# Attention with decay and two feed-forward blocks on one core: weight words to ScalarE, an x product queued behind the q and k remainders, two first-layer products behind the last second-layer product

## The chip, the cores and the metric

The kernel runs on one core of a Trainium2 chip. The metric is the device time of one execution in microseconds, taken over several runs; the profile is one further execution, recorded by the hardware profiler.

## The reference

Four batches of eight heads with 576 positions and 64 features attend causally, with a decay in the exponent; the result goes through two feed-forward blocks. Cut to what matters:

```
scores = q @ k.T / 8 + (cum[i] - cum[j])       # cum = cumsum(log f), causal
attn   = exp(scores - max) / sum               # [4, 8, 576, 576]
x      = (attn @ v) as [2304, 512]
h      = x @ w_in                              # w_in  [512, 2048]
g      = h * tanh(softplus(h))
x2     = g @ w_out                             # w_out [2048, 512]
a, b   = x2 @ w1, x2 @ w2                      # [512, 1024] each
out    = ((a * b) @ w3) @ w_out2               # w3 and w_out2 are multiplied first
```

The weights arrive as 64-bit floats and are handled as pairs of 32-bit words.

## The kernel before

Every float32 product is done in three TensorE passes: an operand is split into a rounded high part and a remainder, and MM_PAIRS (line 60) multiplies high by high, high by remainder and remainder by high. A helper `split` (line 91) makes the two parts; the remainder on POOL (GpSimd) is `pool_sub` (line 102, its instruction is line 108). POOL in the rows is GpSimd, ACT is ScalarE, DVE is VectorE, PE is TensorE with PEld for its weight loads, SP is the queue that issues every DMA.

**Phase A** (`phase_a`, line 685) runs 16 pairs of heads. A pair has nine slots, so there are 144 slots and some more at the end. In a slot the scores of one unit go to PE, the transposes of the unit before it follow, DVE takes the row minimum (line 425), ACT takes the exponential (line 429), and ACT and DVE split the transposed probabilities (lines 502 and 504). In slots 3 and 5 of the next pair the products with v run (`pv`, line 533; `x_rows`, lines 545 and 546; `x_parts`, line 548, whose product with the inverse row sums R is line 551). The heads to come are prepared by `prep_qk` (line 336): ACT copies (lines 348 and 349), then the remainders of k and of q on POOL. v is split by ACT and POOL in `prep_v` (lines 374 and 378).

PE's free time is filled with products that are ready: first w3 times w_out2, later the first layer of the batches that are done (`l1_unit`, line 610; ACT copies the finished bank in line 617 and a DMA stores it, line 618). `plan` (line 663) hands out how many of these go in each slot; `run_filler` queues each behind the slot's scores. A timeline-based scheduler then orders each engine's instructions by readiness and priority, within the bounds that `behind` (an instruction after which something may be issued) and `high_priority` set.

The slots also **convert weights**. A job is: `cv_load` (line 111) issues the load of 512 KB into one of two buffers; `cv_exp` (line 120) multiplies the upper words by a power of two; `cv_bits` (line 134) puts the bits together on DVE (lines 140 to 142); then the tile is split (w3t, w_in) or stored to DRAM (`cv_store`, line 148). Keys are t for w3t, i for w_in, u for w_out and v for w1 and w2. For t and i `cv_exp` is one ScalarE activation of 128x512 (line 132); for u and v it is two GpSimd instructions of 128x256 (line 130). The job's load stands in slot s, `cv_exp` and `cv_bits` in slot s + 1, the store in s + 2 (function `job`, line 734). The u and v jobs begin at slot 72 and come every 2.35 slots.

**Phase B** (`phase_b`, line 978) first runs 16 steps: a step computes g for one feature tile of block 0 (`mish_step`: DVE lines 890, 891 and 896, ACT lines 875 to 884, POOL line 892, the split of g in ACT line 94 and POOL line 108), runs two first-layer products of the last batch (l1[2c] and l1[2c+1]), splits a tile of w1 or w2 (`w12_split`), and runs the second-layer product of the step before (`l2`, line 932). After the last step `l2(15)` closes block 0, `x2_parts` (lines 940 and 941) splits its four banks, and eight blocks of third-layer, second-layer and last products (lines 951, 932 and 971) follow. The third layer takes turns on four PSUM banks, two of which are those of the first layer.

Of the kernel before, what the change touches and what calls it, by code (L numbers as in the profile page):

```python
# [13 lines left out]
AF = mybir.ActivationFunctionType  # L14
ALU = mybir.AluOpType
# [24 lines left out]
HB = 3  # L40
CV = 2
HP_L1 = 50
CV_POOL = "uv"
HP_ATT = 100
HP_SM = 200
HP_PV = 50
# [4 lines left out]
W_OUT_STEP = 2.35  # L51
# [5 lines left out]
W_OUT_SLOT = 72  # L57
# [5 lines left out]
def f32(ap):  # L63
    return ap.bitcast(F32)
# [4 lines left out]
F64_EXP = 2.0 ** -112  # L69
# [3 lines left out]
class Kernel:  # L73
# [28 lines left out]
    def pool_sub(self, lo, raw, hi):  # L102

        n = lo.shape[-1]
        k = -(-n // 320)
        for i in range(k):
            c = slice(n // k * i, n // k * (i + 1))
            self.nc.gpsimd.tensor_tensor(lo[..., c], raw[..., c], f32(hi[..., c]), ALU.subtract)  # L108


    def cv_load(self, key, src, where=None):
# [8 lines left out]
    def cv_exp(self, key):  # L120
        raw = self.cv[key][0]
        if key[0] in "to":
            t = self.x_tile(f"cv{key}", F32)[:, :512]
        else:
            t = self.att.tile([128, 512], F32, name=f"cv{key}", tag="cv", bufs=CV)
        self.cv[key][1] = t
        hw = raw.rearrange("p (n w) -> p n w", w=2)[:, :, 1]
        if key[0] in CV_POOL:
            for c in (slice(0, 256), slice(256, 512)):
                self.nc.gpsimd.tensor_scalar(t[:, c], f32(hw[:, c]), F64_EXP, None, ALU.mult)  # L130
        else:
            self.nc.scalar.activation(t, f32(hw), AF.Copy, scale=F64_EXP)

    def cv_bits(self, key):

# [200 lines left out]
    def prep_qk(self, h, step):  # L336


        nc = self.nc
        raw = self.raw[h]  # L340
        t1, t2 = self.tset(h)
        d0 = 64 if h % 2 else 0
        qs, ks = self.qk_cols(h)
        qd = slice(qs.start + d0, qs.stop + d0)
        kd = slice(ks.start + d0, ks.stop + d0)
        qr, kr = raw[:, h % 2 == 0], raw[:, h % 2]
        if step == 0:
            nc.scalar.copy(t1[:, d0:d0 + 2 * S], raw.rearrange("p w s -> p (w s)"))
            nc.scalar.copy(t2[64:128, qd], qr[64:128])
        elif step == 1:  # L350
            self.pool_sub(t2[64:128, kd], kr[64:128], t1[64:128, kd])
        else:
            self.pool_sub(t1[0:64, qd], qr[0:64], t1[0:64, qd])

    def load_v(self, p):
        nc = self.nc
# [328 lines left out]
    def phase_a(self):  # L685
# [43 lines left out]
        misc, conv = {}, {}  # L729

        def at(s, fn, *a):
            misc.setdefault(s, []).append((fn, a))

        def job(s, key, src, fin, *a):
            at(s, self.cv_load, key, src)
            conv.setdefault(s + 1, []).append(key)
            at(s + 2, fin, *a)

        jobs = [(f"t{f}{q}", self.cols(self.w3t, f, q), self.w3_split, f, q) for f in range(1, 8) for q in range(2)]
        for i, j in enumerate(jobs):  # L740
            job(int(W3_STEP * i), *j)
        jobs = [(f"i{m}", self.cols(self.w_in, m), self.win_split, m) for m in range(DFF // 128)]
        for i, j in enumerate(jobs):
            job(W_IN_SLOT + int(W_IN_STEP * i), *j)
        for i in range(32):
            f = i % 16
            if i < 16:
                key, src, dst = f"u{f}", self.rows(self.w_out, f), self.wo_scr
            else:
                key, src, dst = f"v{f}", self.cols((self.w1, self.w2)[f % 2], f // 2), self.w12_scr  # L750
            job(W_OUT_SLOT + int(W_OUT_STEP * i), key, src, self.cv_store, key, dst[f])
        for p in range(NPAIR):
            s = 9 * p
            if p == 0:
# [20 lines left out]
        for s in range(nslot + 7):  # L775
            if s in L1_S[:3]:
                self.filler.extend(self.l1_all(L1_S.index(s)))
            n = cnt[s]
            with self.tc.high_priority(offset=HP_ATT):
                if s < nslot:  # L780
                    self.pe = self.scores(s)
                if 0 <= s - T_LAG < nslot:
                    self.transposes(s - T_LAG)
                    act = self.pt_parts(s - T_LAG, False)
            if s < nslot:
                with self.tc.high_priority(offset=HP_SM):
                    act = self.softmax_a(s)
            with self.behind(act):
                for key in conv.get(s, []):
                    self.cv_exp(key)  # L790
            k = n // 2
            self.run_filler(k)
            if 0 <= s - T_LAG < nslot:
                with self.tc.high_priority(offset=HP_ATT):
                    dve = self.pt_parts(s - T_LAG, True)
            with self.behind(dve):
                for key in conv.get(s, []):
                    self.cv_bits(key)
            with self.behind(act):
                for fn, a in misc.get(s, []):  # L800
                    fn(*a)
            self.run_filler(n - k)
            if s >= 9:
                p, i = divmod(s - 9, 9)
                with self.tc.high_priority(offset=HP_PV):
                    if i == PV_AT[0]:
                        self.pv(2 * p)
                        self.x_rows(2 * p)
                    elif i == PV_AT[1]:
                        self.pv(2 * p + 1)  # L810
                        self.x_rows(2 * p + 1)
                        self.x_parts(p)
        self.run_filler(len(self.filler))
        self.psp.__exit__(None, None, None)
        self.attp.__exit__(None, None, None)
# [110 lines left out]
    def l2(self, c):  # L926
        f = c % 16
        g = self.g.pop(c)
        mm = self.nc.tensor.matmul
        for e in range(4):  # L930
            for k, (a, b) in enumerate(MM_PAIRS):
                mm(self.xb(e), self.wo[f][:, 512 * a + 128 * e:512 * a + 128 * e + 128],  # L932
                   g[:, TB * b:TB * b + TB], start=f == 0 and k == 0, stop=f == 15 and k == 2)

    def x2_parts(self, j):
        nc = self.nc
        self.x2 = []
        for e in range(4):
            t = self.x_tile(f"x2_{j}_{e}")
            nc.scalar.copy(t[:, :TB], self.xb(e))  # L940
            nc.vector.tensor_tensor(t[:, TB:], self.xb(e), f32(t[:, :TB]), ALU.subtract)
            self.x2.append(t)
# [35 lines left out]
    def phase_b(self):  # L978
        self.hl, self.mt, self.g = {}, {}, {}
        self.late_pool()  # L980
        self.hst = [self.x_tile(f"hst{i}", F32) for i in range(2)]
        l1 = [self.l1_unit(B - 1, m, half) for m in range(16) for half in range(2)]

        def run(steps):
            for _, fn in steps:
                fn()


        for f in range(2):
            self.wout_load(f)  # L990
        for c in range(4):
            self.h_load(c)
        self.m_min(0)
        self.m_exp(0)
        self.m_n(0)
        self.m_min(1)
        for c in range(16):
            self.w12_load(c)
            self.wout_split()
            self.mish_step(c)  # L1000
            run(l1[2 * c])
            if c >= 1:
                self.w12_split()
            run(l1[2 * c + 1])
            if c >= 1:
                self.l2(c - 1)
            if c + 2 < 16:
                self.wout_load(c + 2)
            if c % 2 == 0:
                self.wp_load(c // 2)  # L1010
        self.w12_split()
        self.l2(15)
        self.x2_parts(0)
        for j in range(NBLK):
            self.ab = []
            for f in range(8):
                more = j + 1 < NBLK
                c = 16 * (j + 1) + 2 * f
                if more:
                    self.mish_step(c)  # L1020
                self.l3(j, f)
                self.ab_parts(j, f)
                if more:
                    if f:
                        self.l2(c - 1)
                    self.mish_step(c + 1)
                    self.l2(c)
            if more:
                self.l2(16 * (j + 1) + 15)
            for e in range(4):  # L1030
                self.final(j, e)
                if e == 0 and more:
                    self.x2_parts(j + 1)
# [52 lines left out]
```

## Time and profile before

| | us |
|---|---|
| median of three runs | 1069.72 |
| lowest and highest run | 1068.0, 1072.33 |
| the profiled execution's own time | 1069.25 |
| its span, first to last instruction | 1067.1 |
| PE busy in the span | 965.8 (91%) |
| DVE busy | 770.7 (72%) |
| ACT busy | 633.0 (59%) |
| POOL busy | 598.2 (56%) |

The page cuts the span into 40 equal slices and gives each engine's busy share in tenths, so that a stage shows as a run of digits. Phase A fills about the first 18 of them, the first 16 steps of phase B the next four, the eight blocks the rest. Busy time says how much work an engine has; what a wait costs is read from the rows of the stage in which it stands.

### The profile page before, as it was taken

Reading aid. Unit: us, or ns where it says so; the run is one execution under the profiler, and the core shown is the slowest. Engines: PE = TensorE matmul, PEld = TensorE weight load, DVE = VectorE, ACT = ScalarE, POOL = GpSimd, SP = SyncE. Lnnn points to the kernel's source line nnn. Section 1 sums busy time; section 2 is a strip of 40 time slices with the busy share of each in tenths; the row PEclk is TensorE's granted clock in tenths of the full one; section 3 lists DMA queues with packets and bytes.
Section 4 is the critical chain, followed back from the end, with each engine's and each line's share of the span. In section 5 each row is a group of like instructions: output and inputs, shape, how many; then the busy total and the mean of one; then the engine's idle time right before and its main releaser. Section 6 shows DMA issues by size and latency. Waiting matters only on the chain.

```text
span 1067.1 us, 20221 instructions
## 1 busy us (share of the span) xinstructions
PE 965.8 (91%) x6784; PEld 921.6 (86%) x6784; DVE 770.7 (72%) x1709; ACT 633.0 (59%) x1601; POOL 598.2 (56%) x690
## 2 busy tenths in 40 slices
PE   0788878989998888889988999999999999999998
PEld 0576668979888787888988999999999999999998
DVE  7877767767667676775777886868778696886821
ACT  6778878877777656654655554545445454554511
POOL 5967776686677577655764543535455353543500
PEclk9899999999999989999998999999999999999999
DMA  7757557766767668569552111111211111111000
GB/s 215 182 184 206 147 167 227 205 189 179 228 217 232 192 182 241 182 214 323 190 162 71 41 56 46 45 46 46 62 35 40 56 45 51 41 51 50 18 23 23
DMA packets 107084, 136.36 MB, mean 128 GB/s; under 512 B 11092, under 2 KB 83172, under 8 KB 106980
## 3 DMA queue, kind: packets, MB, share of 16 engines
q1 hardware_dynamic: 106980, 135.07, 42.5%
q8 instruction: 53, 0.87, 0.3%
q14 instruction: 51, 0.42, 0.1%
HBM read 98.39 MB, written 36.54 MB: 126 GB/s over the span
## 4 chain that ended last, share of the span: by engine, by line
PE 53%; DVE 10%; DMA 9%; ACT 7%; issue 5%; POOL 3%; SPq 1%; POOLq 0%; ACTq 0%; DVEq 0%
PE ps_x L932 14%; PE ps_y L951 9%; PE ps_l L610 7%; PE ps_l L951 7%; PE ps_y L971 5%; PE ps_l L971 5%; PE ps_v L533 2%; DMA inv_scr<-inv 2%; DMA cvrv<-in_w_dram 2%; DMA R<-inv_scr 1%; DVE mb L896 1%; DVE cs L890 1%; PE ps_t L465 1%; ACT ma L883 1%; PE ps_s L401 1%
## 5 line engine op out<-in xcount | busy, mean ns | idle before, releaser
L610 PE MATMUL ps_l<-x,wi 128*128 128x288 f32 x1536 | 240.9, 304 | 19.6 <-ACT h L617 7.4
L610 PEld LDWEIGHTS ps_l<-x,wi 128*128 128x128 f32 x1536 | 218.8, 193 | 26.7 <-ACT h L617 9.4
L932 PE MATMUL ps_x<-g,wo 128*128 128x288 f32 x1536 | 223.6, 296 | 1.5 <-POOL g L108 1.5
L932 PEld LDWEIGHTS ps_x<-g,wo 128*128 128x128 f32 x1536 | 210.0, 189 | 4.1 <-POOL g L108 3.2
L108 POOL TENSOR_TENSOR g<-mb,g 128x288 fp32r<-128x288 f32 x128 | 113.8, 889 | 134.4 <-ACT g L94 132.5
L108 POOL TENSOR_TENSOR T<-raw,T 64x288 fp32r<-64x288 f32 x128 | 114.6, 914 | 31.8 <-issue 17.5
L875 ACT ACTIVATE ma<-ma 128x288 f32<-128x288 f32 x128 | 56.5, 442 | 121.6 <-DVE ma L871 121.6
L94 ACT CAST g<-mb 128x288 fp32r<-128x288 f32 x128 | 55.3, 432 | 103.5 <-DVE mb L896 71.2
L951 PE MATMUL ps_y<-x,w 128*128 128x288 f32 x768 | 109.1, 297 | 2.7 <-ACT x L940 1.4
L951 PE MATMUL ps_l<-x,w 128*128 128x288 f32 x768 | 107.9, 295 | 0.0
L951 PEld LDWEIGHTS ps_y<-x,w 128*128 128x128 f32 x768 | 104.9, 191 | 3.2 <-ACT x L940 1.7
L951 PEld LDWEIGHTS ps_l<-x,w 128*128 128x128 f32 x768 | 104.3, 190 | 0.0
L892 POOL TENSOR_TENSOR mb<-mb,hsp 128x288 f32<-128x288 f32 x64 | 62.2, 972 | 68.4 <-issue 29.5
L892 POOL TENSOR_TENSOR mb<-mb,hl 128x288 f32<-128x288 f32 x64 | 63.3, 990 | 65.0 <-DVE cs L890 30.9
L879 DVE SCALAR_TENSOR_TENSOR mb<-ma 128x288 f32<-128x288 f32 x128 | 62.0, 486 | 49.4 <-POOL g L108 49.4
L429 ACT ACTIVATE P<-P,sum 128x128 f32<-128x128 f32 (+3 forms) x144 | 84.9, 590 | 19.1 <-DVE sum L425 15.6
L425 DVE CUSTOM_DVE_ANT_0 P<-ps_s,m 128x384 f32<-128x384 f32 (+3 forms) x128 | 60.9, 481 | 46.0 <-PE ps_t L465 38.7
L504 DVE TENSOR_TENSOR pt<-ps_t,pt 128x128 fp32r<-128x128 f32 (+2 forms) x192 | 74.1, 414 | 25.8 <-ACT pt L502 25.4
L890 DVE SCALAR_TENSOR_TENSOR cs<-mb,ma 128x288 f32<-128x288 f32 x128 | 72.5, 566 | 25.3 <-ACT ma L884 24.9
L891 DVE SCALAR_TENSOR_TENSOR ma<-cs,ma 128x288 f32<-128x288 f32 x128 | 86.8, 678 | 2.5
L533 PE MATMUL ps_v<-pt 128*128 128x320 f32 (+4 forms) x416 | 69.5, 299 | 14.2 <-POOL pt L378 6.0
L533 PEld LDWEIGHTS ps_v<-pt 128*128 128x128 f32 x416 | 62.0, 195 | 21.9 <-POOL pt L378 8.1
(125 smaller groups left out, 1899.7 us busy)
## 6 DMA issues: line engine op xcount, KB each, us to landing
raw<-in_qk_dram SPq DMA_DIRECT2D x64, 288.0 KB
h_scr<-h SPq DMA_DIRECT2D x96, 144.0 KB
hl<-h_scr SPq DMA_DIRECT2D x64, 144.0 KB
hsp<-h_scr SPq DMA_DIRECT2D x64, 144.0 KB
cvrt<-in_w3t_dram SPq DMA_DIRECT2D x16, 512.0 KB
cvri<-in_w_in_dram SPq DMA_DIRECT2D x16, 512.0 KB
cvru<-in_w_out_dram SPq DMA_DIRECT2D x16, 512.0 KB
cvrv<-in_w_dram SPq DMA_DIRECT2D x16, 512.0 KB
```

The source lines that it names most:

```text
L108: self.nc.gpsimd.tensor_tensor(lo[..., c], raw[..., c], f32(hi[..., c]), ALU.subtract)
L429: return nc.scalar.activation(P[:, :n], P[:, :n], AF.Exp, bias=st, scale=-1.0, accum_out=self.sums[:, i:i + 1])
L504: ins = nc.vector.tensor_tensor(self.pt_dst(hd, 1, k, 128 * c, w), a, f32(hi), ALU.subtract)
L533: mm(ps[:, base + q:base + q + w], V[:, kc, :], rhs, start=i == 0, stop=i == n - 1)
L610: mm(o[:, :TB], w, x, start=i == 0, stop=i == 11)
L879: self.nc.vector.scalar_tensor_tensor(b, a, 2.0, a, ALU.add, ALU.mult)
L890: nc.vector.scalar_tensor_tensor(e, b, 2.0, a, ALU.add, ALU.mult)
L891: nc.vector.scalar_tensor_tensor(a, e, 2.0, a, ALU.subtract, ALU.mult)
L892: nc.gpsimd.tensor_tensor(b, b, self.hl[c], ALU.mult)
L932: mm(self.xb(e), self.wo[f][:, 512 * a + 128 * e:512 * a + 128 * e + 128], g[:, TB * b:TB * b + TB], start=f == 0 and k == 0, stop=f == 15 ...
L951: mm(ps, self.w12[f, i][:, 512 * a + 128 * e:512 * a + 128 * e + 128], self.x2[e][:, TB * b:TB * b + TB], start=n == 0, stop=n == 11)
L971: nc.tensor.matmul(ps, self.wp[f][:, 512 * a + 128 * e:512 * a + 128 * e + 128], self.ab[f][:, TB * b:TB * b + TB], start=n == 0, stop=n = ...
```

## The change

1. `cv_exp` gives the upper words of u and v jobs to ScalarE too, in one instruction of 128x512. Their GpSimd branch and its constant go.
2. The u and v jobs get `lag=2`: conversion in slot s + 2 and store in slot s + 3.
3. `x_parts` is issued behind the last instruction of the q remainder that was prepared before it.
4. In the last of the 16 steps of phase B the two first-layer products are left out; they are issued behind the last instruction of `l2(15)`, after `x2_parts(0)` in the text of the program, and the last `w12_split` follows them.

```diff
-CV_POOL = "uv"
...
-        if key[0] in CV_POOL:
-            for c in (slice(0, 256), slice(256, 512)):
-                self.nc.gpsimd.tensor_scalar(t[:, c], f32(hw[:, c]), F64_EXP, None, ALU.mult)
-        else:
-            self.nc.scalar.activation(t, f32(hw), AF.Copy, scale=F64_EXP)
+        self.nc.scalar.activation(t, f32(hw), AF.Copy, scale=F64_EXP)
...
-            self.pool_sub(t1[0:64, qd], qr[0:64], t1[0:64, qd])
+            self.pool_last = self.pool_sub(t1[0:64, qd], qr[0:64], t1[0:64, qd])
...
-        def job(s, key, src, fin, *a):
+        def job(s, key, src, fin, *a, lag=1):
             at(s, self.cv_load, key, src)
-            conv.setdefault(s + 1, []).append(key)
-            at(s + 2, fin, *a)
+            conv.setdefault(s + lag, []).append(key)
+            at(s + lag + 1, fin, *a)
...
-            job(W_OUT_SLOT + int(W_OUT_STEP * i), key, src, self.cv_store, key, dst[f])
+            job(W_OUT_SLOT + int(W_OUT_STEP * i), key, src, self.cv_store, key, dst[f], lag=2)
...
-                        self.x_parts(p)
+                        with self.behind(self.pool_last):
+                            self.x_parts(p)
...
-            run(l1[2 * c])
+            if c < 15:
+                run(l1[2 * c])
             if c >= 1:
                 self.w12_split()
-            run(l1[2 * c + 1])
+            if c < 15:
+                run(l1[2 * c + 1])
...
+        with self.behind(self.l2(15)):
+            self.x2_parts(0)
+            run(l1[30])
+            run(l1[31])
         self.w12_split()
-        self.l2(15)
-        self.x2_parts(0)
```

The line numbers of the changed file are some lines off those of the kernel before. In the rows below xx22 is the attention output of heads 22 and 23, T0 to T2 hold the prepared q and k, va and vb are v, cvv1 is the second tile of the w1 and w2 jobs, cvrv1 its raw words, inv and R the inverse sums.

GpSimd in the kernel before, around the conversion of cvv1 in phase A:

```order
L130 TENSOR_SCALAR cvv0_3972<-cvrv0_3955 128x256 x2
L108 TENSOR_TENSOR T1_93<-raw26_3850,T1_93 64x288 x4
L130 TENSOR_SCALAR cvv1_4052<-cvrv1_4022 128x256 x2
L551 TENSOR_TENSOR xx22_4040<-xx22_4040,R11_3989 128x288 x2
L378 TENSOR_TENSOR pt_91<-va12_3995,pt_91 128x4x64 x2
L378 TENSOR_TENSOR pt_91<-vb12_3996,pt_91 128x2x64
L130 TENSOR_SCALAR cvv2_4152<-cvrv2_4128 128x256 x2
L108 TENSOR_TENSOR x11_0_4106<-xx22_4040,x11_0_4106 128x288
L108 TENSOR_TENSOR x11_1_4110<-xx22_4040,x11_1_4110 128x288
```

In the changed kernel the L130 rows are gone and the others follow each other; the product L551 stood behind the four remainders of raw26 already, and still does. ScalarE in the changed kernel, where cvv1 now stands:

```order
L442 COPY inv11_3903<-ps_t0_85 9x128
L425 ACTIVATE P2_97,sum12_3887<-P2_97,sum12_3887 128x384
L541 COPY xx22_4022<-ps_v_87 64x576
L498 CAST pt_91<-ps_t0_85 128x2x128
L498 CAST pt_91<-ps_t1_86 128x128
L425 ACTIVATE P1_96,sum12_3887<-P1_96,sum12_3887 128x256
L128 ACTIVATE cvv1_4061<-cvrv1_4004 128x512
L613 COPY h1_13_1_4151<-ps_l0_64 128x288
L541 COPY xx22_4022<-ps_v_87 64x576
L498 CAST pt_91<-ps_t0_85 128x2x2x128
L498 CAST pt_91<-ps_t1_86 128x2x128
```

The conversion stands between an exponential and the copy of a first-layer bank; behind it wait that copy and the casts of the transposed probabilities.

TensorE at the end of the 16 steps of phase B, before (wi15 rows are the last first-layer product, g14 and g15 rows the last two of the second layer, w12 rows the third layer):

```order
L610 MATMUL ps_l0_64<-x12_1_4432,wi15_2350 128x288 x3
L610 MATMUL ps_l0_64<-x13_1_4760,wi15_2350 128x288 x3
L610 MATMUL ps_l0_64<-x14_1_5065,wi15_2350 128x288 x3
L610 MATMUL ps_l0_64<-x15_1_5329,wi15_2350 128x288 x3
L932 MATMUL ps_x1_5411<-g14_6381,wo14_6369 128x288 x3
L932 MATMUL ps_x2_5412<-g14_6381,wo14_6369 128x288 x3
L932 MATMUL ps_x3_5413<-g14_6381,wo14_6369 128x288 x3
L932 MATMUL ps_x0_5410<-g15_6447,wo15_6435 128x288 x3
L932 MATMUL ps_x1_5411<-g15_6447,wo15_6435 128x288 x3
L932 MATMUL ps_x2_5412<-g15_6447,wo15_6435 128x288 x3
L932 MATMUL ps_x3_5413<-g15_6447,wo15_6435 128x288 x3
L951 MATMUL ps_y0_5414<-x2_0_0_6512,w12_0_5526 128x288
```

And in the changed kernel:

```order
L929 MATMUL ps_x1_5379<-g15_6415,wo15_6403 128x288 x2
L929 MATMUL ps_x2_5380<-g15_6415,wo15_6403 128x288 x2
L929 MATMUL ps_x3_5381<-g15_6415,wo15_6403 128x288 x2
L606 MATMUL ps_l1_65<-x12_0_4401,wi15_2350 128x288 x3
L606 MATMUL ps_l1_65<-x13_0_4725,wi15_2350 128x288 x3
L606 MATMUL ps_l1_65<-x14_0_5032,wi15_2350 128x288 x3
L606 MATMUL ps_l1_65<-x15_0_5293,wi15_2350 128x288 x3
L606 MATMUL ps_l0_64<-x12_1_4405,wi15_2350 128x288 x3
L606 MATMUL ps_l0_64<-x13_1_4729,wi15_2350 128x288 x3
L606 MATMUL ps_l0_64<-x14_1_5036,wi15_2350 128x288 x3
L606 MATMUL ps_l0_64<-x15_1_5297,wi15_2350 128x288 x3
L949 MATMUL ps_y0_5382<-x2_0_0_6449,w12_0_5494 128x288 x3
```

All 24 wi15 instructions now stand between the last of the second layer and the first of the third; the products of g14 and g15 follow each other without them.

## Rows read from the trace of the kernel before

**Rows 1.** Windows by stage: PE, PEld, DVE, ACT, POOL busy us (instructions), clock, DMA share, GB/s.

```profile
240.00:360.00 120.00, 109.95 (x790) 104.64 (x789) 82.43 (x216) 88.27 (x243) 85.95 (x103) 0.99 0.72 217
360.00:475.00 115.00, 96.40 (x674) 90.41 (x674) 82.25 (x197) 70.42 (x198) 75.06 (x86) 0.97 0.67 199
572.00:1067.00 495.00, 488.95 (x3648) 485.93 (x3648) 355.92 (x775) 229.37 (x567) 201.38 (x223) 0.99 0.15 43
```

**Rows 2.** POOL's waits, 240 to 480 us: releaser, us in total, times, longest us.

```profile
POOL cvv L130 <- DMA cvrv<-in_w_dram: 29.5, 7, 10.4
POOL cvu L130 <- DMA cvru<-in_w_out_dram: 12.8, 4, 4.4
```

**Rows 3.** The chain that ended last, 355 to 440 us: start us, us, what.

```profile
367.65 6.82 DMA cvrv<-in_w_dram
...
398.89 6.43 DMA cvrv<-in_w_dram
...
422.27 4.83 DMA cvrv<-in_w_dram
```

**Rows 4.** PE's timeline, 368 to 436 us: start, us, instructions, idle time before and releaser.

```profile
377.61 0.40 PE L610 MATMUL ps_l<-x,wi 128*128 128x288 f32 x1 [2.25 <-ACT x L94]
379.22 1.12 PE L533 MATMUL ps_v<-pt 128*128 128x256 f32 x4 [1.21 <-POOL pt L378]
...
408.57 0.41 PE L401 MATMUL ps_s<-T 128*128 128x384 f32 x1 [1.69 <-DVE sum L425]
...
430.32 0.80 PE L410 MATMUL ps_s<-T 128*128 128x288 f32 x4 [2.11 <-DVE sum L425]
...
434.78 0.68 PE L533 MATMUL ps_v<-pt 128*128 128x256 f32 x4 [0.83 <-POOL pt L378]
```

**Rows 5.** Windows behind two of PE's gaps, and one of steady work.

```profile
378.30:385.20 6.90, 5.98 (x23) 5.77 (x24) 5.04 (x14) 4.80 (x13) 6.82 (x9) 0.52 0.60 183
...
572.90:579.70 6.80, 5.67 (x23) 5.67 (x24) 6.62 (x14) 2.83 (x6) 3.11 (x4) 0.52 0.17 43
579.70:590.00 10.30, 10.30 (x78) 10.30 (x78) 6.24 (x16) 4.81 (x13) 3.41 (x4) 0.99 0.11 29
```

**Rows 6.** Tile cvv: ns min/median/max, first and last start; its conversion and bits.

```profile
L130 POOL TENSOR_SCALAR cvv<-cvrv x32: 858/870/1297, 358.8 to 470.2; 128x256 f32<-128x256 f32 x32
...
L141 DVE SCALAR_TENSOR_TENSOR cvv<-cvrv,cvv x16: 674/733/1297, 366.4 to 472.1; 128x512 int32<-128x512 int32 x16
L142 DVE SCALAR_TENSOR_TENSOR cvv<-cvrv,cvv x16: 677/748/1307, 367.1 to 473.6; 128x512 int32<-128x512 int32 x16
```

**Rows 7.** Tile cvri, the raw words of w_in: its conversion on ACT and ACT's idle time.

```profile
L132 ACT ACTIVATE cvi<-cvri x16: 661/680/702, 135.9 to 228.0; 128x512 f32<-128x512 f32 x16
...
  DMA cvri<-in_w_in_dram: 1.1, 1
```

**Rows 8.** ACT's longest wait, 240 to 480 us.

```profile
ACT x L94 <- POOL xx L551: 21.2, 9, 4.2
```

**Rows 9.** PE's waits for ACT's casts and copies, 60 to 240 us.

```profile
PE ps_v L533 <- ACT pt L502: 4.0, 4, 1.8
PE ps_l L610 <- ACT h L617: 4.0, 4, 1.3
```

**Rows 10.** PE's waits, 240 to 475 us.

```profile
PE ps_v L533 <- POOL pt L378: 5.3, 5, 1.7
PE ps_s L410 <- DVE sum L425: 5.3, 5, 2.1
PE ps_l L610 <- ACT h L617: 3.4, 4, 1.7
```

**Rows 11.** PE's timeline at the end of phase B's 16 steps.

```profile
567.57 2.94 PE L932 MATMUL ps_x<-g,wo 128*128 128x288 f32 x21
571.94 0.54 PE L951 MATMUL ps_y<-x,w 128*128 128x288 f32 x2 [1.44 <-ACT x L940]
...
574.03 1.81 PE L951 MATMUL ps_y<-x,w 128*128 128x288 f32 x6 [1.29 <-DVE x L941]
```

**Rows 12.** POOL's timeline there: the remainder of g15.

```profile
567.12 1.26 POOL L108 TENSOR_TENSOR g<-mb,g 128x288 fp32r<-128x288 f32 x1
```

More of the change, by code (lines that the diff above doesn't have):

```diff
@@ L107, in pool_sub @@
             c = slice(n // k * i, n // k * (i + 1))
-            self.nc.gpsimd.tensor_tensor(lo[..., c], raw[..., c], f32(hi[..., c]), ALU.subtract)
+            ins = self.nc.gpsimd.tensor_tensor(lo[..., c], raw[..., c], f32(hi[..., c]), ALU.subtract)
+        return ins
     def cv_load(self, key, src, where=None):
@@ L931, in l2 @@
             for k, (a, b) in enumerate(MM_PAIRS):
-                mm(self.xb(e), self.wo[f][:, 512 * a + 128 * e:512 * a + 128 * e + 128],
+                ins = mm(self.xb(e), self.wo[f][:, 512 * a + 128 * e:512 * a + 128 * e + 128],
                    g[:, TB * b:TB * b + TB], start=f == 0 and k == 0, stop=f == 15 and k == 2)
+        return ins
     def x2_parts(self, j):
```

## The prediction

> **What bounds the kernel now.** I read the windows by stage first. From 572 us to the end PE is busy 488.95 of 495 us [rows 1]: there the kernel is bound by TensorE, and the change takes no work from it. What can be won lies before: from 240 to 475 us, which covers the slots of the u and v jobs, PE is busy 109.95 + 96.40 = 206.35 of 235 us [rows 1], so 28.65 us are idle. The waits of POOL come next: it stood 29.5 + 12.8 = 42.3 us, in 11 waits, before a conversion whose load had not landed [rows 2]. POOL takes its instructions in order, so all that is queued behind stood too: the product L551, the remainder of v L378, and on DVE the bits, which need the conversion. The chain of waits then shows that this is no idle time without cost: three loads of cvrv, 6.82 + 6.43 + 4.83 = 18.1 us, lie on the chain that ended last [rows 3]. PE's timeline shows the gaps that follow each of them [rows 4]: 2.25 and 1.21 us after the first (released by the cast of x that had waited for L551, and by L378), 1.69 after the second, 2.11 and 0.83 after the third (two of these by DVE's minimum, queued behind the bits). Last, the windows behind the gaps: after the first, PE had a granted clock of 0.52, nearly its lower level of 1.2 GHz, for 6.9 us [rows 5].
>
> **The change part by part.** The sum is against the profiled execution, 1069.25 us, of which 2.15 lie around its span; that is 0.47 under the median, which I take off nothing.
>
> *Conversions leave POOL.* 64 instructions of 0.87 us, 55.7 us, go [rows 6]. POOL is no bound, so only what stood behind them counts. The five gaps make 2.25 + 1.21 + 1.69 + 2.11 + 0.83 = 8.1 us. They belong to the v jobs with 29.5 us of waits; the u jobs with 12.8 us, at the same rate, give 8.1 x 12.8 / 29.5 = 3.5. The clock window took 5.98 us for 23 matmuls; at the upper level about half of that, 2.9 us, would do [rows 5]. Together **-14.5 us**. Bounds: nothing, if another wait ends just as late, and all 28.65 us of idle time plus the 2.9. I keep 14.5, since each gap has its load on the chain.
>
> POOL's time is where a rule speaks against this part. The rows have 0.87 us for 128x256 on POOL against 0.68 us for 128x512 on ACT [rows 6, 7], so a conversion gets 1.74 - 0.68 = 1.06 us shorter behind a late load. The Trainium skill (GPSIMD Engine Reference, section Engine selection) calls GPSIMD with one input roughly line-rate; at its 1.2 GHz that is an estimate of 0.2 us for 256 elements, so that two would be shorter than ScalarE's one, and each load on the chain would cost 0.25 us more instead of 1.06 less, some 4 us over three v loads. No row here shows it: the fastest of the 32 took 858 ns [rows 6], and the row decides.
>
> *Conversions come to ACT.* 32 x 0.68 = 21.8 us of ACT work come into a stretch in which it is busy 88.27 + 70.42 = 158.7 of 235 us [rows 1]. The cost on PE lies between 0, if it all falls into the 76 idle us (21.2 of them waits for POOL's L551 [rows 8], which get fewer), and 21.8, if every one delays an exponential or cast that PE waits for. The nearest row is the stretch 60 to 240 us, where ACT has 30 conversions and their high parts besides: there PE waited 4.0 + 4.0 = 8.0 us for ACT's casts and first-layer copies, in 180 us [rows 9]; in 240 to 475 us it waited 3.4 for such copies [rows 10]. At the rate of the first, 235 us would have 10.4, so 7 more; half of that for the missing high parts is 3.5. I take **+5**.
>
> *A late load on ACT.* An in-order wait moves from POOL to ACT, and behind it stand the exponential, the casts and the bank copies. Bounds: 0, and the 42.3 us that POOL waited. The nearest row is w_in: 16 loads of the same 512 KB through the same two buffers, converted on ACT one slot after the load, cost ACT 1.1 us [rows 7]. Twice as many, and a slot later each: **+2.2** at most as a forecast. The extra slot also moves the bits and the store; a raw buffer is held one slot longer, but two jobs of 2.35 slots have 4.7, so the next load still finds one free. SP's order keeps each store right ahead of the load that reuses its buffer.
>
> *x's product behind the q remainder.* On POOL, L551 already stands behind the remainders that it is now tied to: 0 us. What covers it is that order alone; were it the other way round, one wait of four remainders, some 3 us, would come with each of 16 pairs.
>
> *The last first-layer products.* PE had l2(15) done at 570.51, then idled 1.44 and 1.29 us around four matmuls until x2 was split [rows 11], and ran 23 matmuls in 5.67 us at the low clock [rows 5]. In steady work one takes 10.30 / 78 = 0.132 us, so 12 take 1.58 and the moved 24 take 3.17. Without these, PE reaches l2(15) at 570.51 - 1.58 - 3.17 = 565.8; but g15's remainder is there only at 567.12 + 1.26 = 568.4 [rows 12]. Four high-by-high products go ahead, eight wait: l2(15) ends at 568.4 + 8 x 0.132 = 569.4, 1.1 us earlier than now. The 24 products then run to 572.6, x2 is split beside them, and the third layer starts without a stop. Before, it ran on from 574.03 with four done, so from 573.5: -0.9 us. So most of the idle time moves ahead of l2(15) instead of going. Whether the clock falls there again I can't tell: it cost 5.67 - 23 x 0.132 = 2.6 us, and I take half, -1.3. Together **-2.2** (bounds: +0.5, and -5.3, all idle time and clock loss).
>
> Sum: -14.5 + 5 + 2.2 - 2.2 = -9.5, so 1059.7, set at **1060 us**.
>
> **The rivals.**
>
> *No change to speak of.* The late loads stop ending the gaps, but the next chain is as late: the inverse sums through DRAM, and DVE, which PE waited 5.3 us for in its minimum alone [rows 10]. With half of the 14.5 us and the same costs: 1069.25 - 7.2 + 5 + 2.2 - 2.2 = 1067. Against it: POOL and DVE both lose a wait. For it: DVE is busy 70% of the stretch [rows 1].
>
> *More gained.* ACT's 21.2 us behind L551 [rows 8] go as well, and DVE gets quicker beside an emptier POOL. The bits have a median of 733 and 748 ns with a fastest of 674 and 677 and a slowest of 1297 and 1307 [rows 6]: something slows them at times. If two thirds of the 28.65 idle us and the clock loss go (22 us), for 5 of costs and 5.3 at the end: about 1047. The Trainium skill (GPSIMD Engine Reference, section Specifications) has GpSimd share its SBUF interfaces with VectorE, with contention for instructions of two SBUF inputs, as L141 and L142 are. The spread of the rows agrees; it does not show what shares the time.
>
> *Slower: ScalarE becomes the bound.* It already carries exponentials, casts and bank copies in order. If each conversion delays PE by its whole 0.68 us, 21.8 us come, and by the late loads 2.2; against 14.5 and 2.2 won it is 1069.25 + 21.8 + 2.2 - 14.5 - 2.2 = 1076.6. It decides from the point at which less than about 12 of the 76 idle us of ACT are free when PE doesn't wait. Against it: 145 to 240 us, where w_in was converted so.
>
> *The change doesn't do what it says.* For x's product that is so, by the order; for the rest the order shows the moves.
>
> **How the numbers follow.** Forecast (1053 to 1064): 0.50. More gained: 0.15. No change: 0.24. Slower: 0.11. About 0.5%, 5.3 us, is what a measurement of this kernel can tell from no change; 1064.4 is the border. So faster 0.65, same 0.25, slower 0.10. The range of **1048 to 1071** leaves out the end of the greater gain and the slower case.
>
> **What would show it.** Right: POOL some 56 us less busy, ACT 22 more; no wait of POOL for a cvr load, few of ACT; PE's idle time from 240 us to the end of phase A down by some 10 us; no clock of 0.5 after the v loads; at the end of the 16 steps a gap before the last eight g15 products instead of two before the third layer. Wrong: ACT's conversions wait several us for their loads, with PE idle in the same us; or PE's gaps stay, released by DVE or by R.

## The result, and the profile after

| | before | after |
|---|---|---|
| median of five runs, us | 1069.72 | 1062.38 |
| lowest and highest | 1068.0, 1076.15 | 1055.64, 1062.95 |
| profiled execution, its span | 1069.25, 1067.1 | 1059.44, 1057.6 |

The ratio, which is taken over all runs, is 0.99, with a 95% interval of 0.9871 to 0.9928: some 10.7 us less. The two medians are 7.3 us apart, so the size is known to a few us only. The profiled execution after lies 2.9 us under its median, so its rows flatter the change a little.

To see where the time went, I cut both traces at the same instructions: from the last scores of heads 14 and 15 (slot 71; the u and v jobs begin at slot 72) to the last scores of phase A. Both pieces hold the same 1331 matmuls. The windows, before and after (from, to, length, then busy us with counts for PE, PEld, DVE, ACT, POOL, then clock, DMA share, GB/s):

```profile
240.97:454.95 213.98, 188.49 (x1331) 178.08 (x1332) 149.83 (x382) 147.18 (x406) 149.85 (x174) 0.98 0.69 206
```

```profile
242.17:449.31 207.14, 187.31 (x1331) 176.92 (x1332) 138.95 (x376) 160.44 (x435) 97.34 (x116) 0.98 0.70 210
```

The piece starts 1.2 us later and is 213.98 - 207.14 = 6.84 us shorter; from its end to the end of the span it is 612.15 before and 608.29 after, 3.86 us less. Together 1.2 - 6.84 - 3.86 = -9.5, the difference of the spans. PE's idle time (length less PE busy) fell from 25.49 to 19.83 us. DVE is 10.9 us less busy in the piece; six instructions fewer fall into it, some 3.8 us by their mean times, and the rest is the same work done faster.

One piece is one execution. The same order of instructions, profiled a second time (e12 below), gave:

```profile
241.55:451.29 209.74, 189.20 (x1331) 177.12 (x1332) 138.40 (x375) 159.40 (x432) 97.70 (x116) 0.98 0.70 208
```

That is 2.6 us longer than the first, and 4.2 instead of 6.84 us shorter than before. Nearly 2 of the 2.6 us are PE's busy time, while DVE's agrees within 0.6 us. So a difference of 2 or 3 us between two pieces says little about PE; of DVE it says more.

The waits of POOL and of ACT, 240 to 480 us, after:

```profile
POOL T L107 <- ACT T L344: 22.2, 5, 6.0
...
POOL xx L547 <- DMA R<-inv_scr: 16.0, 2, 9.1
```

```profile
ACT cvv L128 <- DMA cvrv<-in_w_dram: 13.4, 10, 2.6
ACT x L93 <- POOL xx L547: 10.1, 7, 2.8
ACT cvu L128 <- DMA cvru<-in_w_out_dram: 9.6, 7, 3.1
```

The 42.3 us that POOL stood for loads [rows 2] are gone. But 13.4 + 9.6 = 23.0 us of them now stand on ACT; the cast of x waits 10.1 us for L547 where it waited 21.2 [rows 8]. The tile cvv after (ns min/median/max, first and last start):

```profile
L128 ACT ACTIVATE cvv<-cvrv x16: 653/668/694, 356.0 to 467.1; 128x512 f32<-128x512 f32 x16
...
L137 DVE SCALAR_TENSOR_TENSOR cvv<-cvrv,cvv x16: 673/691/1316, 362.3 to 468.8; 128x512 int32<-128x512 int32 x16
L138 DVE SCALAR_TENSOR_TENSOR cvv<-cvrv,cvv x16: 674/693/1318, 364.3 to 470.4; 128x512 int32<-128x512 int32 x16
```

The same bits had medians of 733 and 748 [rows 6]. PE's timeline after, at its longest stop among the v jobs and at the end of the 16 steps:

```profile
396.34 1.14 PE L406 MATMUL ps_s<-T 128*128 128x288 f32 x4 [2.38 <-DVE sum L421]
...
560.01 0.80 PE L929 MATMUL ps_x<-g,wo 128*128 128x288 f32 x4 [1.46 <-ACT g L93]
561.72 1.32 PE L929 MATMUL ps_x<-g,wo 128*128 128x288 f32 x8 [0.91 <-POOL g L107]
562.87 3.33 PE L606 MATMUL ps_l<-x,wi 128*128 128x288 f32 x24
566.04 3.37 PE L949 MATMUL ps_y<-x,w 128*128 128x288 f32 x24
```

The two stops now stand around g15's first four products, and the third layer starts behind the 24 first-layer matmuls without one. The windows behind those stops:

```profile
396.30:399.80 3.50, 3.46 (x15) 3.46 (x16) 2.52 (x7) 1.49 (x5) 2.32 (x3) 0.54 0.20 64
565.80:576.00 10.20, 10.20 (x80) 10.20 (x79) 8.46 (x20) 5.31 (x14) 3.67 (x4) 1.00 0.25 72
```

Behind the stop of 2.38 us the clock fell to its lower level (0.54 granted); at the end of the 16 steps it did not, in this execution.

### The profile page after: what moved, and what is told of

Its sections match the earlier page's. It is cut to its first block, busy times and chain, and to the rows that moved or that the text cites. A ratio compares the mean times of both kernels' runs of the same rounds, so it can differ in the third digit from the quotient of the medians.

```text
span 1057.6 us, 20180 instructions
## 1 busy us (share of the span) xinstructions
PE 962.2 (91%) x6784; PEld 917.4 (87%) x6784; DVE 761.8 (72%) x1709; ACT 647.5 (61%) x1633; POOL 541.1 (51%) x626
## 5 line engine op out<-in xcount | busy, mean ns | idle before, releaser
L606 PE MATMUL ps_l<-x,wi 128*128 128x288 f32 x1536 | 237.9, 303 | 16.0 <-ACT h L613 7.9
L606 PEld LDWEIGHTS ps_l<-x,wi 128*128 128x128 f32 x1536 | 216.8, 192 | 23.6 <-ACT h L613 10.9
L107 POOL TENSOR_TENSOR T<-raw,T 64x288 fp32r<-64x288 f32 x128 | 112.1, 895 | 66.3 <-issue 34.9
L949 PE MATMUL ps_y<-x,w 128*128 128x288 f32 x768 | 106.8, 294 | 0.0
L888 DVE SCALAR_TENSOR_TENSOR ma<-cs,ma 128x288 f32<-128x288 f32 x128 | 89.6, 700 | 2.4
L529 PE MATMUL ps_v<-pt 128*128 128x320 f32 (+4 forms) x416 | 70.0, 299 | 13.4 <-POOL pt L374 5.0
```

The lines of the kernel that those rows point to most:

```text
L107: ins = self.nc.gpsimd.tensor_tensor(lo[..., c], raw[..., c], f32(hi[..., c]), ALU.subtract)
L529: mm(ps[:, base + q:base + q + w], V[:, kc, :], rhs, start=i == 0, stop=i == n - 1)
L606: mm(o[:, :TB], w, x, start=i == 0, stop=i == 11)
L888: nc.vector.scalar_tensor_tensor(a, e, 2.0, a, ALU.subtract, ALU.mult)
L949: mm(ps, self.w12[f, i][:, 512 * a + 128 * e:512 * a + 128 * e + 128], self.x2[e][:, TB * b:TB * b + TB], start=n == 0, stop=n == 11)
```

## The experiments

All ratios are to the kernel before, timed on the same chip. A us figure is the ratio's distance from 1 times the 1071 to 1072 us of the kernel before there. A piece is cut as above in each trace. The expectations of e1 to e4 count from 1069.7 us, and the kernel before took 1072.15 in their timing, so they are read by their distance from it.

### One part alone

**e1**: only the conversions to ScalarE.

```diff
-        if key[0] in CV_POOL:
...
+        self.nc.scalar.activation(t, f32(hw), AF.Copy, scale=F64_EXP)
```

> The kernel before with the u and v conversions on ScalarE and nothing else (conversion one slot behind the load, as before). Changed against before: 9.5 us less in the profiled execution, 6 of them up to the last scores, nearly all in pairs 13 to 15 where w1 and w2 are converted. Theory (the engine and the extra slot are both needed): the loads land as late as before, so most of the 42.3 us that GpSimd stood before a conversion now stand on ScalarE, with exponentials and casts behind; ScalarE waits 30 us or more for cvr loads and the time is 1066 to 1072, no clear gain. Rival (the engine alone): GpSimd's queue is free, the slot adds nothing; 1063 to 1065, as with both parts, and ScalarE waits no more than the 23 us that the changed kernel shows.

**Slower** by 0.6%: 1.0057 (1.0033 to 1.0081), +6.1 us. The same piece:

```profile
242.84:465.22 222.38, 194.39 (x1331) 182.45 (x1332) 145.03 (x380) 162.50 (x435) 96.72 (x116) 0.95 0.67 199
```

The time comes from two sides: 28.0 us idle, against 25.5 before, and 194.39 us of PE busy for the same matmuls, 5.9 more, at a mean clock of 0.95. The worst stop, in the timelines of PE, ACT, DVE and SP:

```profile
415.18 0.58 PE L397 MATMUL ps_s<-T 128*128 128x256 f32 x1 [4.14 <-DVE sum L424]
...
413.57 0.66 ACT L128 ACTIVATE cvv<-cvrv 128x512 f32<-128x512 f32 x1 [5.27 <-DMA cvrv<-in_w_dram]
414.13 0.71 ACT L425 ACTIVATE P<-P,sum 128x512 f32<-128x512 f32 x1
...
414.26 0.43 DVE L136 TENSOR_SCALAR cvv<-cvv 128x512 int32<-128x512 int32 x1 [4.47 <-ACT cvv L128]
414.60 0.51 DVE L424 CUSTOM_DVE_ANT_0 P<-ps_s,m,sum 128x288 f32<-128x288 f32 x1
...
406.29 1.05 SPq L117 DMA_DIRECT2D cvrv<-in_w_dram  x2
```

SP issued the loads at 406.29; ACT stood 5.27 us for the first, with the exponential behind it; DVE's bits stood 4.47 us behind ACT, with the minimum behind them; PE stood 4.14 us for that minimum. In-order queues put a late load before all three. ACT's waits for loads are 28.1 us here: the theory's 30 was near, but its price was far too low. This is one stop; that late loads made all of the 6.1 us is argued from it, not shown. POOL also stood 34.7 us for the inverse sums R, 9.9 in the kernel before.

**e2**: only the extra slot (`lag=2`), conversions on GpSimd.

```diff
-            conv.setdefault(s + 1, []).append(key)
-            at(s + 2, fin, *a)
+            conv.setdefault(s + lag, []).append(key)
+            at(s + lag + 1, fin, *a)
...
+            job(W_OUT_SLOT + int(W_OUT_STEP * i), key, src, self.cv_store, key, dst[f], lag=2)
```

> The kernel before with the conversion of u and v jobs two slots behind the load, still on GpSimd, and nothing else. Theory (the engine matters): GpSimd still takes 1.74 us for a conversion and waits about 20 us for loads instead of 42.3; about half of the gain of phase A, 1066 to 1068. Rival (the slot alone): the waits for late loads were all that cost, the time is 1062 to 1065, as good as with ScalarE. Second rival (GpSimd's work, not its waits, was in the way): no change, 1069 to 1071.

0.9975 (0.9951 to 0.9998), -2.7 us, on the side of the theory; the interval, 0.2 to 5.3 us less, reaches both rivals. POOL's waits for loads fell from 42.3 to 29.0 us:

```profile
POOL cvu L130 <- DMA cvru<-in_w_out_dram: 17.5, 7, 7.7
POOL cvv L130 <- DMA cvrv<-in_w_dram: 11.5, 6, 3.9
```

So neither part alone brings what both bring in e3.

**e3**: both, the rest as before.

```diff
+        self.nc.scalar.activation(t, f32(hw), AF.Copy, scale=F64_EXP)
...
+            job(W_OUT_SLOT + int(W_OUT_STEP * i), key, src, self.cv_store, key, dst[f], lag=2)
```

> The kernel before with the conversions on ScalarE and two slots behind the load; the last first-layer products stand where they did, and x's product is not tied. Theory: the 6 us up to the last scores come from these two parts, and the end of the 16 steps keeps its two gaps and its low clock: 1062 to 1065. Rival (the last products bring most): 1066 to 1069.

0.9933 (0.991 to 0.9956), -7.2 us, as the theory had it. The slot that is worth 2.7 us on GpSimd is worth 6.1 + 7.2 = 13.3 on ScalarE.

```profile
244.36:450.42 206.06, 187.90 (x1331) 175.77 (x1332) 139.43 (x377) 161.35 (x436) 97.40 (x116) 0.99 0.71 212
...
567.40:574.30 6.90, 5.58 (x23) 5.58 (x24) 6.72 (x13) 2.76 (x6) 3.31 (x4) 0.52 0.14 29
```

The second row is the end of the 16 steps: here, with the last products where they were, the clock fell as in [rows 5].

**e4**: only the last two first-layer products moved.

```diff
-            run(l1[2 * c])
+            if c < 15:
+                run(l1[2 * c])
...
+        with self.behind(self.l2(15)):
+            self.x2_parts(0)
+            run(l1[30])
+            run(l1[31])
...
```

> The kernel before with the last two first-layer products behind the second layer's last product and nothing else. Theory: from the first second-layer product to the end 3 to 4 us less, half of it the clock loss of 2.6 us behind the gaps and half the stops around the first four third-layer products: 1066 to 1067. My forecast had 2.2 for it, 1067.5. Rival (the idle time only moves ahead of g15's products, and the clock falls there instead): 1069 to 1070.

0.9975 (0.9952 to 0.9999), -2.7 us, on the theory's side. The interval, 0.1 to 5.1 us less, leaves out no change by a hair, and it still reaches the rival, which allowed 0.7 us. Its timeline shows the stops of the changed kernel:

```profile
570.49 0.79 PE L932 MATMUL ps_x<-g,wo 128*128 128x288 f32 x4 [1.26 <-ACT g L94]
572.20 1.32 PE L932 MATMUL ps_x<-g,wo 128*128 128x288 f32 x8 [0.91 <-POOL g L108]
573.36 3.33 PE L610 MATMUL ps_l<-x,wi 128*128 128x288 f32 x24
```

**e12**: the changed kernel without the tie of x's product.

```diff
-                        with self.behind(self.pool_last):
-                            self.x_parts(p)
+                        self.x_parts(p)
```

> The changed kernel without the tie of x's product to the q remainder. The order of the instructions is the same on every engine with it and without, so this is the changed kernel once more: ratio 0.987 to 0.993. Rival (the tie does something that the order does not show): outside of that.

0.9888 (0.9859 to 0.9917): no effect of the tie is to be seen, the order of instructions in the two traces is the same on every engine, and so this is a second timing of the change. Its profile holds a lesson. The stops were the same, 1.45 and 0.91 us, but this time the clock fell behind them:

```profile
565.14 1.54 PE L928 MATMUL ps_x<-g,wo 128*128 128x288 f32 x8 [0.91 <-POOL g L107]
566.49 4.68 PE L606 MATMUL ps_l<-x,wi 128*128 128x288 f32 x24
```

4.68 us for the 24 matmuls that took 3.33; the granted clock was 0.53 from 566.2 to 569.7 us. The same order of instructions saved the clock loss in one execution and not in another.

### What ScalarE's work costs

**e5**: each conversion twice.

```diff
+        if key[0] in "uv":
+            self.nc.scalar.activation(t, f32(hw), AF.Copy, scale=F64_EXP)
```

> The changed kernel with each of the 32 u and v conversions written twice, one after the other, on ScalarE (the second repeats the first): 21.4 us more work of ScalarE between 240 and 475 us, no more loads. Against the kernel before the change is worth 10.7 us (ratio 0.99). My forecast charged 5 us for the first 21.8 us of conversions. If that term was right, or low, a second 21.4 us cost as much or more: 4 to 8 us of the 10.7 are given back, 6 to 3 are left (ratio 0.994 to 0.998). Rival (ScalarE's idle time swallows them): under 2 us given back, ratio 0.990 to 0.992. Second rival (every conversion holds up PE by its whole time): 21 us given back, slower than before by 1%.

0.9995 (0.9973 to 1.0016): 10.2 to 11.5 us given back, by the change's two timings, for 21.4 us of work. That is more than the 4 to 8 us expected and half of what the second rival had.

```profile
243.14:462.83 219.69, 194.46 (x1331) 183.08 (x1332) 139.95 (x376) 175.67 (x462) 96.44 (x116) 0.95 0.68 200
```

Idle time is 25.2 us, 5.4 more than after; PE busy 194.46, 7.2 more, at 0.95. Against the piece of e12 it is 4.7 and 5.3. So about half of the loss is PE running slower, not PE waiting.

**e9**: no conversion at all. The exponent's top bit needs no arithmetic, so the bits can start from the raw words.

```diff
+TOP2 = -(1 << 30)
...
-        self.nc.scalar.activation(t, f32(hw), AF.Copy, scale=F64_EXP)
+        if key[0] not in "uv":
+            self.nc.scalar.activation(t, f32(hw), AF.Copy, scale=F64_EXP)
...
-        dve.tensor_scalar(ti, ti, 3, 0x7FFFFFF8, ALU.logical_shift_left, ALU.bitwise_and)
-        dve.scalar_tensor_tensor(ti, w[:, :, 1], SIGN, ti, ALU.bitwise_and, ALU.bitwise_or)
+        new = key[0] in "uv"
+        dve.tensor_scalar(ti, w[:, :, 1] if new else ti, 3, 0x3FFFFFF8 if new else 0x7FFFFFF8,
+                          ALU.logical_shift_left, ALU.bitwise_and)
+        dve.scalar_tensor_tensor(ti, w[:, :, 1], TOP2 if new else SIGN, ti, ALU.bitwise_and, ALU.bitwise_or)
```

> The changed kernel without any conversion of the upper words of u and v: the bits on DVE take them straight from the raw words. Shifted left by 3 and cut with 0x3FFFFFF8 (not 0x7FFFFFF8) the lower bits of the exponent are right, and its top bit already stands at bit 30, so the second of the three bit operations copies two bits (sign and exponent's top) instead of one. ScalarE loses 32 x 0.67 = 21.4 us, GpSimd gets nothing; DVE's first bit operation reads every other word and may take up to the 0.69 us of the second, instead of 0.42, 9 us in all. A second set of conversions cost 10.2 us (ratio 0.9995 against 0.99). Theory (conversions on ScalarE cost about half of their time, the first set as the second): another 4 to 10 us won, ratio 0.980 to 0.986. My forecast's 5 + 2.2 us for the first set would give 0.983. Rival (the first set falls into ScalarE's idle time, only the second hurts): ratio 0.988 to 0.991, or above it by DVE's longer operation.

0.988 (0.9855 to 0.9905): 1 to 2 us better than the change's two timings, which this can't tell from nothing.

```profile
243.05:450.17 207.12, 184.66 (x1331) 176.68 (x1332) 144.32 (x379) 146.82 (x406) 97.64 (x117) 0.98 0.71 212
```

ACT lost 13.6 us against after in the piece, DVE got 5.4 busier, though its first bit operation did not get longer (a median of 428 ns on cvu, 418 after). The waits moved too: DVE now stood 7.1 us for loads, and POOL 34.4 us for R, 16.0 after. So the first set's price isn't separated here: the rival fits, and so does a higher price that DVE and these waits took back.

**e11**: e9's bits for every weight, and no conversion of any; the edit against e9:

```diff
-        if key[0] not in "uv":
+        if key[0] not in "uvtio":
...
-        new = key[0] in "uv"
+        new = key[0] in "uvtio"
```

> e9's bit operations for every weight (w3t, w_in and the first eight of w_out too): all ScalarE conversions are gone, some 40 more of 0.67 us, 27 us of ScalarE work before 240 us, where it was busy 143.7 of 180 us. Theory (as for e9, half their time): 5 to 13 us beyond e9, ratio 0.970 to 0.980. Rival (DVE, whose first operation gets longer by up to 0.27 us each, is the bound there): no more than e9, 0.980 to 0.986, or above it.

0.9953 (0.9933 to 0.9974), 7.8 us worse than e9, the rival's side and beyond. By the profiles about half is lost at the start: the piece begins 5.1 us later than in e9. The first 60 us, here and in the kernel before:

```profile
0.00:60.00 60.00, 18.34 (x65) 13.62 (x66) 47.35 (x85) 29.73 (x65) 39.29 (x55) 0.96 0.59 172
```

```profile
0.00:60.00 60.00, 28.49 (x109) 21.01 (x109) 47.94 (x101) 42.92 (x91) 44.40 (x61) 0.91 0.71 202
```

DVE is as busy, ACT 13 us less, and PE has done 65 matmuls instead of 109 (99 in e9). The largest new stop of PE:

```profile
30.43 0.76 PE L402 MATMUL ps_s<-T 128*128 128x256 f32 x2 [17.71 <-DMA T<-pt]
```

These scores wait for rows that are made from the decay on DVE. With no conversion to wait for, the bits of two weights run on DVE among the operations of the decay: line 233 starts at 15.34 us instead of 8.49, line 251, which makes the first of the rows, at 20.99 instead of 14.87, and the scores at 30.43 instead of 26.79. So the start is lost on DVE, and in part by what comes first in its queue. What ScalarE's time is worth there e11 does not show.

### Waits or work on GpSimd

**e8**: idle work on GpSimd in the place of the old conversions, tied to the slot's exponential.

```diff
+        if key[0] in "uv":
+            for c in (slice(0, 256), slice(256, 512)):
+                self.nc.gpsimd.tensor_scalar(self.dup[:, c], self.dup[:, c], self.last_p[:, 0:1], None, ALU.min)
...
```

> The changed kernel with idle work on GpSimd in the place of the removed conversions: in the same 32 slots two tensor_scalar of 128x256 on a tile of their own, which wait for the slot's exponential and for no load, and which nobody waits for; about 55 us of GpSimd work. Theory (the late loads in front of GpSimd's queue cost, not its work): at most 2 us given back, ratio 0.990 to 0.992. Rival (GpSimd's work beside DVE slows the bits, and takes its place in the queue): 4 us or more given back, ratio 0.994 or above, with L137 and L138 back at medians of 733 and 748 ns from 691 and 693.

0.9979 (0.9958 to 1.0): 8 to 10 us given back; my theory, that only waits cost, fell. The bits of cvv had medians of 729 and 810 ns. But the probe brought a wait of its own:

```profile
POOL dup L131 <- ACT P L430: 33.9, 12, 10.9
...
DVE P L426 <- POOL dup L131: 7.9, 4, 2.9
```

**e10**: as many instructions of the same size, with no wait for another engine.

```diff
+                with self.behind(self.plast):
+                    self.plast = self.nc.gpsimd.tensor_scalar(self.dup[:, c], self.dup[:, c], 1.0, None, ALU.mult)
...
```

> The changed kernel with idle work on GpSimd, two tensor_scalar of 128x256 per u and v job on a tile of their own, now with no wait for any other engine: they are only issued behind GpSimd's instruction before them. e8 had the same work with a wait for the slot's exponential, and DVE's minimum waited 7.9 us for it. Theory (GpSimd's work itself costs, by its place in the queue and by DVE's slower bits beside it): 5 us or more given back of 10.7, ratio 0.995 or above. Rival (e8's loss came from the waits that it brought): under 2 us, ratio 0.990 to 0.992. Between them, both have a part.

0.9938 (0.9907 to 0.9969): 4 to 5 us given back, between the two. Its interval still touches those of the change's two timings; on the same chip its seven runs have a median of 1066.45 us, the six of e12 1060.92. Its tile dup, and its piece:

```profile
L132 POOL TENSOR_SCALAR dup<-dup x64: 839/848/1296, 252.3 to 473.9; 128x256 f32<-128x256 f32 x64
```

```profile
243.78:456.43 212.65, 191.31 (x1331) 178.45 (x1332) 143.44 (x376) 160.50 (x435) 148.52 (x174) 0.98 0.69 205
```

The work makes DVE 143.44 - 138.95 = 4.5 us busier in the same instructions. DVE's groups in the piece (busy us, mean ns, then idle time before), after and in e10, show where:

```profile
L137 DVE SCALAR_TENSOR_TENSOR cvu<-cvru,cvu 128x512 int32<-128x512 int32 x16 | 11.1, 695 | 0.2
L500 DVE TENSOR_TENSOR pt<-ps_t,pt 128x256 fp32r<-128x256 f32 x48 | 19.5, 418 | 11.3 <-ACT pt L498 11.0
```

```profile
L141 DVE SCALAR_TENSOR_TENSOR cvu<-cvru,cvu 128x512 int32<-128x512 int32 x16 | 13.7, 863 | 0.2
L506 DVE TENSOR_TENSOR pt<-ps_t,pt 128x256 fp32r<-128x256 f32 x48 | 19.5, 418 | 10.6 <-ACT pt L504 10.2
```

All bits of u and v together took 61.1 us instead of 56.5, the whole growth, and 3.6 of the 4.6 stand in the operations with two inputs in SBUF, the on-chip memory; instructions that read PSUM, the banks TensorE writes to, kept their times. It falls unevenly: the third bit operation on cvu kept its 784 ns. The Trainium skill (GPSIMD Engine Reference, section Specifications) has GpSimd and VectorE share their SBUF interfaces, with contention for instructions of two SBUF inputs; these rows agree.

No engine waited longer for POOL, so what stood behind the added work in its queue is not what cost: between 240 and 480 us ACT's cast of x waited 4.0 us for POOL, 10.1 after, and PE 3.0 us, 4.7 after. How DVE's 4.5 us reached PE is not shown: PE's idle time in the piece is 21.3 us, 19.8 after and 20.5 in e12, and the rest of the longer piece is PE's busy time. The 4 to 5 us are more than half of what the conversions' move brought (7.2 us in e3), with intervals of some 2 to 4 us on either.

### Two tries for more

**e6**: one slot more.

```diff
-dst[f], lag=2)
+dst[f], lag=3)
```

> The changed kernel with the conversions three slots behind their loads. In the changed kernel ScalarE still stood 23.0 us before conversions whose load had not landed, in 17 waits, and one slot more (lag 1 to 2) was worth 13 us on ScalarE. Theory (the rest of these waits still costs): ScalarE's waits for loads fall under 8 us and 2 to 5 us more are won, ratio to before 0.985 to 0.988. Rival (the raw buffers are held a slot longer, so the next load starts later by as much): waits of 15 us or more stay, and the ratio is 0.990 to 0.994.

0.9944 (0.9923 to 0.9964), 5 to 6 us worse than the change's two timings, on the rival's side. ACT's waits for loads fell only from 23.0 to 16.9 us; the product with R got late instead, 40.0 us of POOL's waits against 16.0 after:

```profile
POOL xx L547 <- DMA R<-inv_scr: 40.0, 4, 14.7
...
ACT cvv L128 <- DMA cvrv<-in_w_dram: 10.4, 10, 2.5
...
ACT cvu L128 <- DMA cvru<-in_w_out_dram: 6.5, 6, 2.2
```

Why R came later with a slot more I did not settle, nor whether that made e6 slower: e9 had 34.4 us of the same waits and lost nothing.

**e7**: only the last first-layer product held back.

```diff
-            if c < 15:
-                run(l1[2 * c])
+            run(l1[2 * c])
...
-            run(l1[30])
```

> The changed kernel with only the last first-layer product, not the last two, behind the second layer's last one; the other runs in step 15 as before. In the changed kernel PE stood 1.46 and 0.91 us around four products of g15, and 24 first-layer matmuls (3.3 us) covered the splits of x2. Theory: the 12 matmuls of 1.6 us put ahead fill most of the 2.4 us; the 12 left cover about half of the 2.7 us that x2's splits take, so 1 us of idle time comes back before the third layer: between 1 us won and 1 us lost, a ratio of 0.989 to 0.991. Rival (the clock falls again behind that stop, as in the kernel before, 2.6 us): ratio 0.992 to 0.993.

0.9898 (0.9877 to 0.9918), no difference, as expected. The stop before g15 went from 1.46 to 0.21 us, and one of 0.61 came back before the third layer:

```profile
564.61 0.80 PE L929 MATMUL ps_x<-g,wo 128*128 128x288 f32 x4 [0.21 <-ACT g L93]
566.30 1.32 PE L929 MATMUL ps_x<-g,wo 128*128 128x288 f32 x8 [0.91 <-POOL g L107]
...
570.27 1.05 PE L949 MATMUL ps_y<-x,w 128*128 128x288 f32 x6 [0.61 <-DVE x L939]
```

## Why the prediction was right, and where it was not

The forecast was 1060 us, 9.5 less than the profiled execution; the median fell to 1062.38, and the two timings give 10.7 and 12.0 us. The sum and its split held: 7.3 for phase A, where e3 measured 7.2 (4.7 to 9.6), and 2.2 for the end, where e4 measured 2.7 (0.1 to 5.1). Inside phase A the terms are less sure, and that their sum came out is in part luck.

- **Conversions leave POOL, -14.5: the reason was half of it.** I charged all five gaps to waits for late loads and gave DVE nothing. e2 took 13 of the 42.3 us of waits away for 2.7 us; e10 put back work alone, without a wait for another engine, and lost 4 to 5, with DVE's bits slower by as much. So DVE's relief, which I had only in the rival "more gained", is likely part of the gain. And the u jobs, to which I gave 3.5, brought nothing to be seen: the last scores of heads 14 and 15 run 1.2 us later than before, those of heads 22 and 23 1.4; the whole gain came behind them, among the v jobs.
- **Conversions come to ACT, +5: only bounded.** e9 takes away the conversions and ACT's waits for loads together, 7.2 us by my sum, and won 1 to 2 us; what its busier DVE and its longer waits for R took back is not known. e5 puts a second set at 10.2 to 11.5. Five fits between these. If it is less, POOL's 14.5 was too high by as much, since e3 fixes the sum of these terms.
- **A late load on ACT, +2.2: this step failed.** I took w_in's 1.1 us [rows 7], converted one slot after its load, as the nearest row; the u and v loads made ACT stand 23.0 us at two slots, 28.1 at one (e1). What the 23.0 us cost on PE no run separates; in the changed kernel no such wait is longer than 3.1 us, in e1 the longest is 5.3. At one slot the slower rival comes true with the same conversions on ScalarE, so not by their work, as I had it, but by when they stand in its queue.
- **The rival "slower" was mispriced.** By its own terms the kernel gets slower when the conversions cost more than 14.5 us, so when less than about 7 of ACT's 76 idle us are free, not 12.
- **x's product: right, 0.** The order said so, and e12 agrees.
- **The last products, -2.2: right, with its mechanism.** The idle time moved ahead of g15's products and x2 is split beside the 24 matmuls. I had one gap, before the last eight products; there are two, 1.46 us before the first four, which wait for ACT's high part of g15, and 0.91 before the eight. I took half of the clock loss since I couldn't tell; one execution shows it gone, another of the same order shows it back (e12).
- **What was to be seen.** POOL 57 us less busy on the page (598.2 to 541.1): right. ACT in the windows of [rows 1] 88.27 + 70.42 to 97.33 + 82.02, 20.7 more: right. PE's idle time down by 10 us: 5.7. No low clock among the v jobs: wrong, once, at 396 us. Few waits of ACT for loads: wrong.

## What to carry to other kernels

Moving work to another engine moves its wait too, and all that is queued behind it: ask first when the data lands, and put the consumer late enough before it goes into a fuller queue; e1 and e3 differ by that alone, by 13 us. Later is not always better: one slot more was worse (e6). An engine that nobody waits for can still cost, and while it works another one can be slower: put back its work without its waits, and see (e10). When a stage gets longer, split the loss into PE's idle time and PE's busy time over the same matmuls: in e1 more than half and in e5 about half was PE running slower, at a mean clock of 0.95 instead of 0.98. And profile one order of instructions twice before you read 2 us out of one trace.

## What was not expected of the hardware

GpSimd's work that touches only a tile of its own, 64 instructions of 848 ns, added 4.5 us to DVE's busy time in unchanged instructions, all of it in the bits of u and v, which read SBUF (e10). And one order of instructions, with the same two stops of 1.45 and 0.91 us ahead, ran its next 24 matmuls in 3.33 us in one execution and, at a granted clock of 0.53 for the first 3.5 us or so, in 4.68 in another (after, e12): the lower level (1.2 GHz of 2.4) is not decided by the order alone.
